# Ending the local softmax inside its own attention step, with the exponentials ahead of the probability transposes

## The chip, the cores and the metric

One Trainium2 chip, one core of it. The metric is the device time of one launch, in microseconds, as the median of several runs; lower is better. A profile is one further execution, taken by the hardware profiler.

## The reference

An attention layer of 4 batches, 8 heads, 576 positions and head dimension 64 is followed by two mixture-of-experts layers on its 2304 rows of 512 numbers. The attention has two parts that are added: a local one, in which a position sees the positions less than 4 away, and a coarse one on means over 4 positions.

```python
q_d = q.reshape(B, H, Sd, 4, D).mean(axis=3)            # k_d and v_d alike, Sd = 144
out_up = np.repeat(sm_attn(q_d, k_d, v_d), 4, axis=2)
mask = np.abs(pos[:, None] - pos[None, :]) < 4
scores = np.where(mask, scale * q @ k.T, -1e9)
attn = softmax(scores)                                   # denominators get + 1e-9
x = out_up + attn @ v                                    # then two MoE layers, top 2 and top 1
```

## The kernel before

The program is written for a manual schedule: each engine executes its instructions in the order in which the Python code issues them. It has an attention stage, a short passage to the experts, and the two expert layers, which are almost all matrix multiplication.

The attention runs as a software pipeline over 16 pairs of heads, in a loop of 18 steps (L1104). In step i it works on four pairs at once. In the order of issue:

- `transposes(i+1)`: TensorE turns queries and keys (tiles `pq`, `pk`); VectorE sums them over 4 positions (`qd`, `kd`), ScalarE copies them out (`qT`, `kT`).
- `softmax2(i-1)`: VectorE sums the local exponentials (`sm`) and takes reciprocals, for the coarse sums (`smd`) too; GpSimd multiplies three of the four bands into the block matrix `Pd`, VectorE one; GpSimd scales the coarse probabilities `ped`.
- `values(i-2)` on TensorE (tiles `pva`, `pvm`), and `scale_d`, ScalarE's copy `od`.
- In some steps `xback_att` (tile `px`), which turns 128 finished rows back. It stands ahead of the scores in steps 6, 7, 10, 11, 14 and 15 and at the end of steps 6, 7, 9, 10, 11, 13 and 14.
- `scores(i)`: 90 small matmuls into the tile `pd`, local ones first, coarse ones last. Then `combine(i-2)` on VectorE (`xT`).
- `p_transposes(i-1)`, first half: TensorE turns the 10 blocks of `Pd` into three tiles `pp`, which ScalarE copies to `pT`.
- `softmax1(i)`: VectorE takes the maximum `mx` and subtracts it (`pe`), ScalarE takes the exponential.
- `p_transposes(i-1)`, second half: 8 transposes of `ped` into two tiles `ppd`, and their copies `pdT`.
- `softmax_d1(i)`, in every second step `group(g+1)` (tile `prs`), and `softmax_d2(i)`: the coarse maximum `mxd` on VectorE and four exponentials on ScalarE.
- `pool_v`: three additions on GpSimd for the coarse values `vd`.

The tiles `pq`, `pk`, `pva`, `pvm`, `pp`, `ppd` and `prs` all come from one pool of PSUM with four buffers (tag `P`), so each one has to wait for the readers of the tile that was taken four places before it:

```python
self.ps = ctx.enter_context(tc.tile_pool(name="attP", bufs=4, space=PSUM))   # L63
pp = self.ps.tile([128, 4, 128], F32, tag="P", name="pp")                    # L281
```

Score tiles and `px` share a second pool of two. From step 12 on, the first router's work on VectorE, GpSimd and TensorE (`route1`) is fed in between: every VectorE instruction of the attention is followed by `tick(1)`, which issues the router's next piece, such as the comparisons `ol` (L526, GpSimd) and `oh` (L527, VectorE), which the matmuls of L532 multiply. After step 17 come the last five `px`, their stores to DRAM, and the first expert.

Of the kernel before, what the change touches and what calls it, by code (L numbers as in the profile page):

```python
# [15 lines left out]
ALU = mybir.AluOpType  # L16
# [28 lines left out]
class Attention:  # L45
# [208 lines left out]

    def softmax2(self, i):
        nc, NB, W, KW, sb = self.nc, self.NB, self.W, self.KW, self.sb
        st = self.st[i]
        pe, ped, smd = st["pe"], st["ped"], st["smd"]
        Pd = self.Pd[i % 2]
        sm = sb.tile([128, 2 * NB], F32, tag="sm", name="sm")  # L260
        self.V.tensor_reduce(sm, pe, axis=AX.X, op=ALU.add)
        self.V.tensor_scalar(sm, sm, 1e-9, None, op0=ALU.add)
        self.V.reciprocal(sm, sm)
        self.V.tensor_scalar(smd, smd, 1e-9, None, op0=ALU.add)
        for g in (1, 2, 3, 0):
            n = KW if g < 3 else W
            s = slice(W * g, W * (g + 1))
            eng = self.V if g == 0 else nc.gpsimd
            eng.tensor_tensor(Pd[s, :, W * g:W * g + n], pe[s, :, :n],  # L269
                              sm[s, :, None].to_broadcast([W, 2 * NB, n]), op=ALU.mult)  # L270
        self.V.reciprocal(smd, smd)
        nc.gpsimd.tensor_tensor(ped, ped, smd[:, :, :, None].to_broadcast([72, 2, 2, self.Sd]), op=ALU.mult)

# [99 lines left out]
def finish_now(gen):  # L373

    while True:
        try:
            next(gen)
        except StopIteration as e:
            return e.value
# [155 lines left out]
class Items:  # L535
# [87 lines left out]
    def next(self):  # L623

        nc, w, tag, nt = self.nc, self.consts, self.tag, self.nt
        m = w.tile([128, self.most], F32, tag=f"{tag}nm", name="nm")
        j = w.tile([128, self.most], F32, tag=f"{tag}nj", name="nj")
        r = w.tile([128, 1 + nt], F32, tag=f"{tag}nr", name="nr")
        ei = w.tile([128, 1], I32, tag=f"{tag}nei", name="nei")
        nc.vector.tensor_scalar(m, self.ij, self.count, None, op0=ALU.is_equal)  # L630
        for a, src in enumerate([self.ei] + [self.col[:, a] for a in range(nt)]):
            nc.vector.tensor_tensor(j, m, src, op=ALU.mult)
            nc.vector.tensor_reduce(r[:, a:a + 1], j, axis=AX.X, op=ALU.add)
        nc.vector.tensor_copy(ei, r[:, 0:1])
        nc.vector.tensor_scalar(self.count, self.count, 1.0, None, op0=ALU.add)
        return dict(e=ei[0:1], e128=r[:, 0:1], col=[r[:, 1 + a:2 + a] for a in range(nt)])
# [219 lines left out]
def core(ctx, tc, q, k, v, moe_w_gate, moe_w_noise, moe_noise, moe_w1, moe_w2,  # L856
         moe2_modality_id, moe2_w_gate, moe2_modality_bias, moe2_w1, moe2_w2, out):
    nc = tc.nc
# [40 lines left out]
    with ExitStack() as actx:  # L899
        att = Attention(actx, tc, q, k, v, identF, xpool)  # L900
# [64 lines left out]
        def flush():  # L965
            while after:
                after.pop(0)()

        def xback_att(t):
            px = att.psD.tile([128, 2, 512], F32, tag="D", name="px")  # L970
            pv = px[:, :, :2 * XB].rearrange("p a (b c) -> p a b c", b=2)
            xr = xback(t, [pv[:, 0], pv[:, 1]])

            def rest():
                nc.scalar.activation(xr, pv[:, :, :, :128], AF.Copy)
                lgs = axr.tile([128, 2, 2, 2 * E], F32, tag="lgs", name="lgs")
                nc.scalar.activation(lgs, pv[:, :, :, 128:], AF.Copy)
                nc.vector.tensor_reduce(lg[:, t], lgs.rearrange("p a b c -> p c a b"), axis=AX.XY, op=ALU.add)
                nc.scalar.dma_start(x_rows[128 * t:128 * t + 128, :DM], xr.rearrange("p a b c -> p (a b c)"))
            after.append(rest)  # L980
# [62 lines left out]
        def tick(n=1, pe=False):  # L1043

            if pe:
                wait[0] = False
            while n and back and not wait[0]:
                n -= 1
                try:
                    what = next(back[0])  # L1050
                    wait[0] = what in ("PE", "PE soon") and not pe
                    age[0] = 2 if what == "PE soon" else 0
                except StopIteration:
                    back.pop(0)

        def unblock(lag=0):

            if wait[0]:
                if age[0] < lag:
                    age[0] += 1  # L1060
                else:
                    wait[0] = False
                    tick(1)
# [20 lines left out]
        def places_early():  # L1084

            v, f = (t.rearrange("p (e t) -> p e t", e=E)[:, :NX, :NE0] for t in (tab, fs))
            yield from rt.decode(f, v, rt.padh.rearrange("p (e t) -> p e t", e=E)[:, :NX, :NE0])
            nc.vector.tensor_copy(idx0[:, 0], f)

            d = route.tile([128, NX, NE0], F32, tag="hold2", name="hold2")  # L1090
            nc.vector.tensor_scalar(d, f, float(N), -float(N), op0=ALU.is_ge, op1=ALU.mult)
            yield
            nc.vector.tensor_tensor(idx0[:, 1], d, f, op=ALU.add)
            yield

        att.tick = tick
        NP = 4 * B
# [6 lines left out]
        for i in range(NP + 2):  # L1104
            g, ph = divmod(i, 2)
            if ph == 1:
                if g + 1 < 2 * B:
                    att.load_vr(g + 1)
                if g + 2 < 2 * B:
                    att.load_qk(g + 2)  # L1110
            if ph == 0 and i and g < 2 * B:
                att.load_vw(g)
            if 3 <= i <= 7:
                next(small, None)
            if i == NP - 1:
                att.pool_v(g, 1)
            if i + 1 < NP:
                if i == 0:
                    att.scores(i)
                    att.softmax1(i)  # L1120
                tr = att.transposes(i + 1)
                next(tr)
            if 1 <= i <= NP:
                att.softmax2(i - 1)
            if i + 1 < NP:
                finish_now(tr)
            if i >= 2:
                att.values(i - 2)
                att.scale_d(i - 2)
            flush()  # L1130
            if i == 12:
                back.append(route1(0, HT, att_bank, nc.vector, nc.gpsimd, hold))
                back.append(places_early())
            unblock(1)
            if i in before:
                xback_att(before[i])
            if 0 < i < NP:
                att.scores(i)
            if i >= 2:
                att.combine(i - 2)  # L1140
            flush()
            tick(2)
            if 1 <= i <= NP:
                pt = att.p_transposes(i - 1)
                next(pt)
            if 0 < i < NP:
                att.softmax1(i)
            if 1 <= i <= NP:
                finish_now(pt)
            unblock(1)  # L1150
            if i < NP:
                att.softmax_d1(i)
                if ph == 0 and g + 1 < 2 * B:
                    att.group(g + 1)
                att.softmax_d2(i)
                for c in ((0,), (1,))[ph] if i > 1 else ((), (0, 1))[ph]:
                    if i < NP - 1:
                        att.pool_v(g, c)
            tick(2 if i < NP else 30)
            if i == 9:  # L1160
                second_bias()
            if i in behind:
                xback_att(behind[i])
            if i == 12:

                nc.sync.dma_start(x_rows[N:].rearrange("(a p) c -> p a c", p=128),
                                  zero[:, None, :].to_broadcast([128, 5, XW]))
            if i == 14:
                ffn.begin([dict(e=e, ns=n, w1=moe_w1, w2=moe_w2) for e, n in
                           [(e, EARLY) for e in range(NX)] + [(e, 640 - EARLY) for e in range(NX)]  # L1170
                           + [(e, 640) for e in range(NX, E)]]
                          + [dict(ns=n, w1=moe2_w1, w2=moe2_w2) for n in [512, 256, 256, 384] + [256] * (STATIC - 1)])

                nc.sync.dma_start(x2_rows.rearrange("(a p) c -> p a c", p=128),
                                  zero[:, None, :YW].to_broadcast([128, NT + 5, YW]))
# [490 lines left out]
```

## Time and profile before

| what | value |
|---|---|
| median of 3 runs | 917.04 us (916.91 to 917.12) |
| the profiled execution | 912.9 us, span 911.2 us |
| TensorE busy in the span | 861.5 us (95%) |
| VectorE, ScalarE, GpSimd busy | 544.4, 431.3, 324.7 us |
| attention (to about 163 us): TensorE, VectorE, ScalarE, GpSimd busy | 137.36, 123.70, 98.16, 121.95 us |
| mean granted TensorE clock | 0.981 of 2.4 GHz |

Busy time is the time in which an engine executes. The profiled execution is one of its own, 4.1 us below the median of the runs. A wait is put down to the engine and the line whose result came last.

### The profile page before, as it was taken

What the parts mean: (1) busy time and instruction counts of PE and PEld (TensorE: products, weight loads), DVE (VectorE), ACT (ScalarE), POOL (GpSimd) and SP (SyncE); (2) the same over time, 40 slices, a digit from 0 to 9 for tenths busy, and PEclk for the clock granted to TensorE, in tenths of its full rate; (3) what the DMA queues carried; (4) which work ended last, traced back from release to release, by engine and by line L of the source; (5) the groups of instructions that cost most, each with busy time, mean ns of one, the idle gap of its engine ahead of it and who ended that gap; (6) DMA issues with size and microseconds to landing.
All of it is one profiled execution on the core that took longest, in us unless ns stands there. A gap on an engine that the chain in (4) does not pass through costs nothing. (4 is left out here: it accounts for less than half of the span.)

```text
span 911.2 us, 18186 instructions
## 1 busy us (share of the span) xinstructions
PE 861.5 (95%) x6775; PEld 757.3 (83%) x6775; DVE 544.4 (60%) x1317; ACT 431.3 (47%) x967; POOL 324.7 (36%) x460
## 2 busy tenths in 40 slices
PE   5898987799999999999999999989989999999995
PEld 4777876688889989999999989978867889999995
DVE  5776887489865544553343443434666877556662
ACT  3676764455554434443342333334324456455562
POOL 7767768265532304224015051050020442222210
PEclk9999998899999999999999999999999999999998
DMA  7978897675776647466237264184424477556660
GB/s 167 178 149 200 203 287 248 205 227 159 247 240 170 162 142 204 122 210 160 74 99 162 88 110 148 47 191 157 147 63 131 142 249 244 185 179 214 212 208 24
DMA packets 158701, 153.82 MB, mean 169 GB/s; under 512 B 74319, under 2 KB 119887, under 8 KB 158608
## 3 DMA queue, kind: packets, MB, share of 16 engines
q1 hardware_dynamic: 142336, 113.33, 41.0%
q0 software_dynamic: 12080, 32.45, 15.5%
q10 hardware_dynamic: 4192, 6.82, 2.1%
q8 instruction: 56, 0.92, 0.4%
q14 instruction: 37, 0.30, 0.1%
HBM read 124.98 MB, written 27.85 MB: 168 GB/s over the span
## 5 line engine op out<-in xcount | busy, mean ns | idle before, releaser
L728 PE MATMUL ph<-xh,whi 128*128 128x256 f32 (+3 forms) x768 | 238.3, 310 | 4.6 <-ACT xh L713 2.4
L728 PE MATMUL ph<-xl,whi 128*128 128x256 f32 (+3 forms) x768 | 237.3, 309 | 0.5 <-DVE xl L714 0.5
L728 PE MATMUL ph<-xh,wlo 128*128 128x256 f32 (+3 forms) x768 | 237.3, 309 | 0.4 <-DVE wlo L689 0.3
L740 PE MATMUL y<-whi,hh 128*128 128x512 f32 x472 | 191.0, 405 | 0.0
L689 DVE TENSOR_TENSOR wlo<-raw,whi 128x512 fp32r<-128x512 f32 x135 | 93.3, 691 | 158.7 <-ACT whi L688 146.0
L740 PE MATMUL y<-wlo,hh 128*128 128x512 f32 x472 | 187.0, 396 | 0.0
L740 PE MATMUL y<-whi,hl 128*128 128x512 f32 x472 | 186.4, 395 | 0.1
L688 ACT ACTIVATE whi<-raw 128x512 fp32r<-128x512 f32 x160 | 101.0, 631 | 167.6 <-PE y L740 149.8
L728 PEld LDWEIGHTS ph<-xh,whi 128*128 128x128 f32 x768 | 145.7, 190 | 14.1 <-ACT xh L713 3.1
L728 PEld LDWEIGHTS ph<-xl,whi 128*128 128x128 f32 x768 | 145.7, 190 | 8.4 <-DVE xl L714 1.1
L730 ACT ACTIVATE hh<-ph 128x256 fp32r<-128x256 f32 (+3 forms) x192 | 83.3, 434 | 141.0 <-PE ph L728 130.2
L728 PEld LDWEIGHTS ph<-xh,wlo 128*128 128x128 f32 x768 | 145.8, 190 | 2.3 <-DVE wlo L689 0.8
L731 DVE SCALAR_TENSOR_TENSOR hl<-ph,hh 128x256 fp32r<-128x256 f32 (+3 forms) x192 | 92.5, 482 | 85.0 <-ACT hh L730 82.4
L1208 POOL DMA_INDIRECT x_rows<-y,idx x35 | 57.8, 1652 | 207.3 <-ACT y L1199 107.3
L691 DVE TENSOR_TENSOR wlo<-raw,whi 128x512 fp32r<-128x512 f32 x160 | 119.4, 746 | 12.5 <-ACT whi L690 11.3
L740 PEld LDWEIGHTS y<-whi,hl 128*128 128x128 f32 x472 | 88.8, 188 | 21.6 <-DVE wlo L691 0.5
L740 PEld LDWEIGHTS y<-whi,hh 128*128 128x128 f32 x472 | 89.4, 189 | 13.2 <-DVE y L1201 0.2
L690 ACT ACTIVATE whi<-raw 128x512 fp32r<-128x512 f32 x160 | 98.7, 617 | 1.9 <-DMA raw<-in_moe_w_dram 1.9
L740 PEld LDWEIGHTS y<-wlo,hh 128*128 128x128 f32 x472 | 89.2, 189 | 12.5
L714 DVE TENSOR_TENSOR xl<-pt,xh 128x512 fp32r<-128x512 f32 x59 | 38.6, 687 | 33.3 <-ACT xh L713 33.1
L1208 POOL DMA_INDIRECT out_dram<-y,pi x19 | 20.6, 1085 | 99.7 <-ACT y L1199 43.9
L269 POOL TENSOR_TENSOR Pd<-pe,sm 32x380 f32<-32x380 f32 (+1 forms) x48 | 42.4, 884 | 31.4 <-DVE smd L40 19.5
(304 smaller groups left out, 1073.8 us busy)
## 6 DMA issues: line engine op xcount, KB each, us to landing
raw<-in_moe_w_dram SPq DMA_DIRECT2D x156, 512.0 KB
x_rows<-zero SPq DMA_DIRECT2D x1, 5934.0 KB
vr<-in_v_dram SPq DMA_DIRECT2D x16, 288.0 KB
x2l<-x_rows SPq DMA_DIRECT2D x18, 256.0 KB
qk<-in_q_dram SPq DMA_DIRECT2D x32, 128.0 KB
qk<-in_k_dram SPq DMA_DIRECT2D x32, 128.0 KB
x_rows<-xr ACTq DMA_DIRECT2D x13, 256.0 KB
vw<-in_v_dram SPq DMA_DIRECT2D x24, 128.0 KB
```

Of the source, the lines that this page charges most:

```text
L269: eng.tensor_tensor(Pd[s, :, W * g:W * g + n], pe[s, :, :n], sm[s, :, None].to_broadcast([W, 2 * NB, n]), op=ALU.mult)
L688: nc.scalar.activation(h1, a, AF.Copy)
L689: eng.tensor_tensor(l1, a, h1.bitcast(F32), op=ALU.subtract)
L690: nc.scalar.activation(hi[:, 1], r2[:, half], AF.Copy)
L691: nc.vector.tensor_tensor(lo[:, 1], r2[:, half], hi[:, 1].bitcast(F32), op=ALU.subtract)
L714: nc.vector.tensor_tensor(xl, p, xh.bitcast(F32), op=ALU.subtract)
L728: nc.tensor.matmul(ps, w[a][:, k], x[b][:, k, s], start=(i == 0), stop=(i == 3 * KD - 1))
L730: nc.scalar.activation(hh[:, s], ps, AF.Relu)
L731: nc.vector.scalar_tensor_tensor(hl[:, s], ps, 0.0, hh[:, s].bitcast(F32), op0=ALU.max, op1=ALU.subtract)
L740: nc.tensor.matmul(p, h[a][:, 128 * j:128 * j + 128], w[b], start=(f == 0 and i == 0), stop=(f == self.FB - 1 and i == 2))
L1208: d = nc.gpsimd.indirect_dma_start(out=dst, out_offset=bass.IndirectOffsetOnAxis(ap=ix, axis=0), in_=y, in_offset=None, **kw)
```

## The change

The local part of `softmax2`, which stood near the beginning of the next step, is issued at the end of its own step, behind `softmax_d1`. What it did for the coarse part becomes a function of its own, which stays near the beginning of the next step. `softmax1` is issued ahead of the whole of `p_transposes`, so that on ScalarE the local exponential of pair i stands ahead of the copies `pT` of pair i-1. `pool_v` moves from the end of a step to a place behind the scaling of `ped`.

```diff
     def softmax2(self, i):
...
         self.V.reciprocal(sm, sm)
-        self.V.tensor_scalar(smd, smd, 1e-9, None, op0=ALU.add)
         for g in (1, 2, 3, 0):
...
+
+    def softmax_d3(self, i):
+        nc = self.nc
+        ped, smd = self.st[i]["ped"], self.st[i]["smd"]
+        self.V.tensor_scalar(smd, smd, 1e-9, None, op0=ALU.add)
         self.V.reciprocal(smd, smd)
         nc.gpsimd.tensor_tensor(ped, ped, smd[:, :, :, None].to_broadcast([72, 2, 2, self.Sd]), op=ALU.mult)
...
-            if i == NP - 1:
-                att.pool_v(g, 1)
...
             if 1 <= i <= NP:
-                att.softmax2(i - 1)
+                att.softmax_d3(i - 1)
+            if 0 < i < NP:
+                for c in ((0,), (1,))[ph] if i > 1 else (0, 1):
+                    att.pool_v(g, c)
...
             tick(2)
+            if 0 < i < NP:
+                att.softmax1(i)
             if 1 <= i <= NP:
                 pt = att.p_transposes(i - 1)
                 next(pt)
-            if 0 < i < NP:
-                att.softmax1(i)
             if 1 <= i <= NP:
                 finish_now(pt)
             unblock(1)
             if i < NP:
                 att.softmax_d1(i)
+                att.softmax2(i)
                 if ph == 0 and g + 1 < 2 * B:
                     att.group(g + 1)
                 att.softmax_d2(i)
-                for c in ((0,), (1,))[ph] if i > 1 else ((), (0, 1))[ph]:
-                    if i < NP - 1:
-                        att.pool_v(g, c)
```

## Rows read from the trace of the kernel before

**Rows 1.** Busy us (x instructions) of PE, PEld, DVE, ACT, POOL; clock, DMA share, GB/s.
```profile
0.00:163.00 163.00, 137.36 (x2525) 117.40 (x2525) 123.70 (x345) 98.16 (x330) 121.95 (x182) 0.96 0.83 205
...
180.00:911.00 731.00, 712.02 (x4182) 629.09 (x4180) 414.28 (x959) 326.78 (x624) 199.28 (x266) 0.99 0.54 160
```
**Rows 2.** Waits of TensorE, 12 to 145 us: total, times, longest.
```profile
PE pp L283 <- POOL Pd L269: 9.0, 8, 2.4
...
PEld prs L166 <- ACT pT L284: 0.6, 2, 0.4
```
**Rows 3.** Timeline of step 3 (start us, duration us, engine, line).
```profile
31.07 0.66 PE L193 MATMUL pq<-gw,qk 128*128 128x128 f32 x4
...
34.42 2.77 POOL L269 TENSOR_TENSOR Pd<-pe,sm 32x380 f32<-32x380 f32 x3 [2.22 <-DVE smd L40]
...
37.25 1.31 PE L283 MATMUL pp<-gw,Pd 128*128 128x128 f32 x10 [1.55 <-POOL Pd L269]
...
39.09 0.66 PE L193 MATMUL pq<-gw,qk 128*128 128x128 f32 x4
```
**Rows 4.** Timeline of step 7: its beginning and its last part.
```profile
64.06 0.60 PE L193 MATMUL pq<-gw,qk 128*128 128x128 f32 x4
...
68.84 0.71 PE L222 MATMUL pd<-kd,qd 64*72 64x144 f32 x8
69.49 1.31 PE L283 MATMUL pp<-gw,Pd 128*128 128x128 f32 x10
69.60 0.55 DVE L40 TENSOR_REDUCE mx<-pd 128x10 f32<-128x380 f32 x1 [0.66 <-PE pd L222]
...
70.26 0.55 DVE L40 TENSOR_TENSOR pe<-pd,mx 128x380 f32<-128x380 f32 x1
...
70.63 0.67 PE L292 MATMUL ppd<-gw,ped 72*72 72x72 f32 x8
...
71.14 1.19 PE L955 MATMUL px<-gw,xT 128*128 128x144 f32 x8
...
71.36 0.53 ACT L233 ACTIVATE pe<-pe 128x380 f32<-128x380 f32 x1
...
71.77 0.71 ACT L294 ACTIVATE pdT<-ppd 72x288 f32<-72x288 f32 x2
```
**Rows 5.** Instructions that write `pT`: duration in ns, min/median/max.
```profile
L284 ACT ACTIVATE pT<-pp x48: 367/571/580, 20.8 to 153.4; 128x488 f32<-128x488 f32 x32, 128x244 f32<-128x244 f32 x16
```
**Rows 6.** Busy time and granted clock (PEclk) by stretch of the attention.
```profile
64.10:72.20 8.10, 8.10 (x162) 7.35 (x161) 6.67 (x18) 5.92 (x22) 5.37 (x7) 1.00 0.75 151
31.00:106.10 75.10, 69.06 (x1395) 59.12 (x1393) 57.16 (x145) 51.52 (x182) 55.52 (x70) 1.00 0.86 184
111.10:123.60 12.50, 9.69 (x166) 8.06 (x167) 12.36 (x38) 6.74 (x22) 8.70 (x11) 0.93 0.88 241
121.90:125.30 3.40, 3.40 (x21) 3.37 (x19) 3.33 (x10) 1.52 (x4) 2.31 (x4) 0.50 0.81 178
```
**Rows 7.** Timeline of steps 1 and 2.
```profile
19.63 2.40 PE L283 MATMUL pp<-gw,Pd 128*128 128x128 f32 x10 [3.59 <-DVE mxd L40]
...
25.45 0.47 PE L309 MATMUL pva<-pdT,vd 72*64 72x144 f32 x4 [1.16 <-POOL vd L181]
```
**Rows 8.** Timeline of steps 12 and 13, with the router's work in between.
```profile
120.90 1.97 PE L283 MATMUL pp<-gw,Pd 128*128 128x128 f32 x10 [2.39 <-POOL Pd L269]
...
123.58 0.54 DVE L40 TENSOR_REDUCE mx<-pd 128x10 f32<-128x380 f32 x1
...
124.95 0.52 ACT L233 ACTIVATE pe<-pe 128x380 f32<-128x380 f32 x1 [1.64 <-DVE pe L40]
...
125.49 0.60 PE L193 MATMUL pq<-gw,qk 128*128 128x128 f32 x4
```
**Rows 9.** Timeline of the change from step 15 to step 16.
```profile
146.07 0.69 ACT L294 ACTIVATE pdT<-ppd 72x288 f32<-72x288 f32 x2
...
146.51 1.28 PE L309 MATMUL pva<-pdT,vd 72*64 72x144 f32 x7 [2.02 <-ACT pdT L294]
```

More of the change, by code (lines that the diff above doesn't have):

```diff
@@ L256, in softmax2 @@
         nc, NB, W, KW, sb = self.nc, self.NB, self.W, self.KW, self.sb
-        st = self.st[i]
-        pe, ped, smd = st["pe"], st["ped"], st["smd"]
+        pe = self.st[i]["pe"]
         Pd = self.Pd[i % 2]
```

## The prediction

> **What bounds the kernel now.** I read the busy time by stretch first. From 180 us to the end TensorE is busy 712 of 731 us [rows 1], and the change touches nothing there: whatever the attention gains or loses arrives at the end unchanged. In the attention TensorE idles 26 of 163 us [rows 1]; that is all there is to win. The table of waits says for what it idles: 9.0 us, eight times, for `Pd` from GpSimd [rows 2]. The timelines show the place. In step 3 `pq` starts at 31.07; its sum `qd` and, behind it in VectorE's queue, the sums and reciprocals of `softmax2` let GpSimd start `Pd` only at 34.42, 2.77 long; `pp` starts at 37.25 after 1.55 idle, and the next `pq` at 39.09 [rows 3]. So the loop is `pq`, `qd`, `sm`, `Pd`, `pp`, `pq`: 8.02 us. Steps that also carry `px` have the extra matmuls to hide it: from 64.1 to 72.2 TensorE is busy all the time [rows 6]. Over steps 3 to 11 (31.0 to 106.1) it idles 75.1 - 69.06 = 6.0 us in nine steps [rows 6].
>
> **The change part by part.**
>
> *What it removes.* `Pd` of pair i is started by GpSimd at the end of step i. It needs 2.8 us, and the next step's `pp` comes only after transposes, values and scores, over 4 us of TensorE. All waits of `pp` for `Pd` go, and those for `vd`, as `pool_v` comes earlier in the step. No instruction is added or taken away: the same three `Pd` products, one `ped` product and three additions of `pool_v`, the same VectorE instructions and ticks, the same DMAs. SP's queue keeps its order; `pool_v` ends earlier, so buffers for the next `vr` come free earlier, not later.
>
> *What it adds.* On ScalarE the exponential of pair i now stands ahead of the copies `pT` of pair i-1, and it waits for scores, maximum and subtraction of pair i. Queued behind it: three `pT`, two `pdT`, the four coarse exponentials, the next `kT`, `qT`, `od`. TensorE waits for these through the four PSUM buffers. The order in the pool is `pq pk pva pvm pp pp pp ppd ppd` (`prs`): the second `ppd` takes the buffer of the first `pp`, so it waits for the first `pT`; the next `pq` waits for the second `pT` (behind a `prs`, for the third). That the pool works so is seen now: `prs` waited for `pT` twice [rows 2].
>
> *The new wait, from step 7* [rows 4]. Let S be the end of the scores, 68.84 + 0.71 = 69.55. `mx` starts 0.05 later, `pe` 0.66 after it, 0.55 long; the exponential could start at S + 1.3 (now it starts at 71.36 because the copies are ahead of it). The next ScalarE instruction starts 0.41 after an exponential (71.36 to 71.77), and a first `pT` takes 0.57 [rows 5]: done at S + 2.3, so the second `ppd` starts at S + 2.35. TensorE is there at S + 1.4: `pp` at 69.49, `ppd` at 70.63, half of which is 0.3. It stalls 0.95 us, or 1.05 where `pq` or `prs` follows at once and waits for the next copy. The price falls in every step, also in those in which TensorE never waited. It lies between nothing (other work ready in the queue: there is none, the queue is in order) and this 0.95 to 1.05.
>
> *Is something else the loop then?* From S: stall and `ppd` to S + 2.7, `pq` at S + 2.8 (S + 3.2 with `prs`), and from `pq` to the next S 4.5 us (64.06 to 69.55 is 5.5, with 1.1 of `px` [rows 4]). That is 7.3 and 7.7 us against 8.02 now in step 3. ScalarE's chain from the exponential to `od`, and `combine` behind it, comes to S + 7.1 or 7.4, just inside. So the plain steps gain a little and the steps with `px` lose.
>
> *Sum, in the profiled execution's time.*
> Steps 0 to 2: `pp` waits 3.59 now [rows 7]; `Pd` can start about 1 us earlier, as the two sums of `group` and one `qd` (0.7) no longer stand ahead of it on VectorE. GpSimd's queue is full behind it, so the `vd` for which `values` of step 2 wait [rows 7] comes 1 us earlier too, and the new stall takes most of that: -0.2 (bounds -1.5 to +0.5).
> Steps 3 to 11: nine stalls, 9.2 us in all, for 6.0 of idle now: +3.1; the `vd` waits stretch some matmuls that count as busy, three times about 0.3: +2.1 (bounds -1.5, with half the stall, to +3.1).
> Steps 12 and 13: between the two maxima of pairs 12 and 13 VectorE is busy 12.36 of 12.50 us [rows 6], and its instructions between them are the same before and after, with as many ticks. So the second maximum doesn't come earlier. Now `pq` starts 1.91 after it (123.58 to 125.49), as `pp` and most of `ppd` are done [rows 8]. After the change the second `ppd` waits for it: exponential at +1.37 [rows 8], `pT` done at +2.35, then 0.3 and a `px` of 1.1 us: `pq` at +3.8, or 1.9 later. TensorE would stand idle for about 5 us ahead of that. After the idle of 2.39 us at this place the granted clock was 0.50, that is 1.2 GHz, for 3.4 us [rows 6, 8]; then it fell on `pp` and `ppd` ahead of the maximum, and would now fall on `px` behind it, another 1.3. I take +2.5 (bounds 0 and +3.2).
> Step 14: the router's matmuls stand behind the `ppd` and come 1.1 us later; VectorE waits for them: +1.1 (bounds 0 and +1.1).
> Steps 15 to 17: the first `pva` waits 2.02 us for `pdT` [rows 9], which now is next behind the exponential on ScalarE; with three `pT` between (1.2 us) it starts that much later. The router's last comparisons on GpSimd wait for matmuls behind that `pva`: +1.1 (bounds -3, if GpSimd, relieved of one `Pd`, ends earlier, and +1.2).
> Together -0.2 + 2.1 + 2.5 + 1.1 + 1.1 = +6.6: 912.9 becomes 919.5. The median of the runs is 4.1 above the profiled execution: 923.6.
>
> *The skill.* The rows show one wait of TensorE repeating from step to step, for `Pd` [rows 2, 3], and a full pool behind it only as 0.6 us. The Trainium skill, Perfetto Trace Analysis, Optimization Strategy, says that a gap which keeps repeating on the engine that should be saturated can mean that there is not enough PSUM for the next tile. The trace doesn't bear this out for the kernel before; it would for the one after. The same section also advises to make the producer of such a gap start sooner: by that alone the gaps are gain and the time is the 907 of the first rival.
>
> **The rivals.**
> *Faster: the stall at the second `ppd` does not come.* It decides at one point: whether the first `pT` is done by S + 1.4. That needs a pool that gives the second `ppd` a free buffer. For it: the waits for `Pd` are real, and the step would then be limited by the rest of the loop. Gain: 9.0 for `Pd` in eight places [rows 2], 1.2 for `vd` [rows 7], 1.7 for 3.4 us at half clock, less about 2 that ScalarE's chain keeps: 10, so 907. Against it: the wait of `prs` for `pT`.
> *No change: the stall comes, the router's steps don't lose.* VectorE is what sets steps 12 to 16 (12.36 of 12.50); if TensorE's lateness is caught up there, as the next maximum waits for VectorE anyway, only -0.2 + 2.1 remain, and a GpSimd that ends earlier in the tail gives some of it back: about 917 to 919. For it: VectorE idles little; against it: the maximum of pair 14 waits for TensorE.
> *Slower still: the longer idles cost the clock in several places*, each 1.7 us as in the 3.4 us at 0.50 [rows 6], in steps 13, 15 and 16: 928.
>
> **How the numbers follow.** Forecast, +3 to +9: 0.56, time 923.6, its own range 920 to 926. Faster rival: 0.24 (the waits removed are measured, the added one is derived). No change: 0.15. Slower still: 0.05. A difference under 0.2%, 1.8 us, can't be told from none with this kernel's runs. The forecast and the slowest case make slower 0.61, and 0.01 of the middle case joins them; 0.13 of the middle case is within the bound and 0.01 below it: faster 0.25, same 0.13, slower 0.62. The range leaves out the better half of the faster rival: 908 to 928.
>
> **What would show it.** In the profile after: no wait of `pp` for `Pd`; instead `ppd` waiting for `pT`, about 0.9 us in nearly each of 15 steps; `pT` starting right behind the exponential; TensorE idle in each of steps 6, 7, 10 and 11, which have none or little now; the distance of `pq` to `pq` near 7.3 in steps 3 and 5 and above 9 in step 7; after the maximum of pair 13 `pq` over 3.5 us later. The prediction is wrong if `ppd` waits for nothing, or if VectorE reaches the second maximum of the router's steps earlier than 12.5 us after the first.

## The result, and the profile after

The median went from 916.77 us (16 runs) to 921.38 us (16 runs): ratio 1.0055, 95% interval 1.004 to 1.0069, so the change costs about 5 us of 917. That lies in the forecast's own range of 920 to 926. The profiled execution after took 921.21 us (span 919.5), the one before 912.9 (span 911.2).

The two profiled executions therefore differ by 8.3 us where the medians differ by 4.6. That of after lies at its median, that of before 3.9 under its own. A stage's loss in the table further down is a difference of these two executions, and 3.7 us of all the losses together are chance that can't be put into one stage.

TensorE's waits after, from 12 to 150 us (total, times, longest; the view of [rows 2]):

```profile
PE ppd L295 <- ACT pT L287: 13.3, 14, 2.7
PE pp L286 <- DVE kd L40: 2.1, 1, 2.1
PE pva L312 <- POOL vd L181: 2.0, 1, 2.0
```

The 9.0 us of waits for `Pd` [rows 2] are gone, and 13.3 us of waits for `pT` stand in their place: one of 0.84 us in nearly every step, and a long one among the router's work. The waits removed were eight; those added are fourteen. Step 7, with `px`, the counterpart of [rows 4], shows one of them being made:

```profile
71.72 0.56 DVE L40 TENSOR_REDUCE mx<-pd 128x10 f32<-128x380 f32 x1 [0.66 <-PE pd L222]
71.77 1.15 PE L286 MATMUL pp<-gw,Pd 128*128 128x128 f32 x9
...
72.38 0.55 DVE L40 TENSOR_TENSOR pe<-pd,mx 128x380 f32<-128x380 f32 x1
...
72.75 0.41 PE L295 MATMUL ppd<-gw,ped 72*72 72x72 f32 x4
...
72.97 0.52 ACT L233 ACTIVATE pe<-pe 128x380 f32<-128x380 f32 x1 [2.20 <-DVE pe L40]
73.39 1.29 ACT L287 ACTIVATE pT<-pp 128x488 f32<-128x488 f32 x3
...
74.01 0.45 PE L295 MATMUL ppd<-gw,ped 72*72 72x72 f32 x4 [0.84 <-ACT pT L287]
...
74.29 1.19 PE L958 MATMUL px<-gw,xT 128*128 128x144 f32 x8
...
74.88 1.97 POOL L267 TENSOR_TENSOR Pd<-pe,sm 32x380 f32<-32x380 f32 x2 [3.16 <-DVE sm L40]
...
75.32 0.60 PE L193 MATMUL pq<-gw,qk 128*128 128x128 f32 x4
```

Read it along one matrix. `mx` and `pe` run on VectorE while TensorE transposes `pp` and the first half of `ppd`. ScalarE idles 2.20 us, since the exponential heads its queue and has no input yet; only behind it, at 73.39, does the first `pT` copy start, though its `pp` had long been written. The second half of `ppd` waits for that copy, `px` and the next `pq` stand behind it on TensorE. `Pd` is now made at the end of the step, in good time.

The busy windows answer [rows 1] and the last lines of [rows 6] (busy us of PE, PEld, DVE, ACT, POOL; clock, DMA share, GB/s):

```profile
0.00:163.00 163.00, 132.61 (x2450) 112.08 (x2452) 119.85 (x327) 92.66 (x316) 116.35 (x176) 0.95 0.80 200
180.00:919.50 739.50, 721.05 (x4239) 637.45 (x4238) 419.32 (x969) 331.23 (x634) 198.59 (x267) 0.99 0.53 161
...
114.50:127.20 12.70, 9.40 (x176) 7.55 (x170) 12.37 (x39) 5.58 (x20) 7.93 (x10) 1.00 0.75 213
128.40:135.00 6.60, 6.16 (x38) 5.83 (x40) 3.59 (x12) 4.41 (x17) 4.06 (x5) 0.50 0.98 306
```

TensorE is as full behind 180 us as before (97.5% after, 97.4% before), so the loss is the attention's; there it idles 30 us of the first 163 instead of 26. Among the router's steps VectorE is again full (12.37 of 12.70), and then come 6.6 us at a granted clock of 0.50, 1.2 GHz, against 3.4 us in [rows 6]. They begin at the end of this wait, the counterpart of [rows 8]:

```profile
126.43 0.54 DVE L40 TENSOR_REDUCE mx<-pd 128x10 f32<-128x380 f32 x1
...
128.22 1.29 ACT L287 ACTIVATE pT<-pp 128x488 f32<-128x488 f32 x3
...
128.84 0.70 PE L295 MATMUL ppd<-gw,ped 72*72 72x72 f32 x4 [2.68 <-ACT pT L287]
...
129.32 2.22 PE L958 MATMUL px<-gw,xT 128*128 128x144 f32 x8
...
131.34 1.06 PE L193 MATMUL pq<-gw,qk 128*128 128x128 f32 x4
```

Here `px` took 2.22 us where it takes 1.19 at the full clock (71.14 in [rows 4]), and `pq` came 4.9 us behind the maximum; before, 1.91 [rows 8]. But before, this `px` had run in the slow stretch too: it started at 123.62 and took 2.03 us. Of the 3.0 us by which `pq` comes later, 2.85 are the wait of `ppd` and its transposes, and 0.15 the longer `px`.

By stages, from the same marks in both traces (start of `pq`, of `mx`, of the last block of `px`):

| stage | before, us | after, us | difference | forecast |
|---|---|---|---|---|
| to `pq` of step 3 | 31.07 | 34.09 | +3.0 | -0.2 |
| `pq` of step 3 to `pq` of step 12 | 75.06 | 76.69 | +1.6 | +2.1 |
| `pq` of 12 to `pq` of 14 | 19.36 | 20.56 | +1.2 | +2.5 |
| `pq` of 14 to `mx` of pair 15 | 18.94 | 18.66 | -0.3 | +1.1 |
| `mx` of 15 to the last `px` block | 12.31 | 16.06 | +3.7 | +1.1 |
| behind it | 754.46 | 753.44 | -1.0 | 0 |

The middle came as forecast or milder; the two ends, which the forecast had nearly level, lost most. How far one trace can be trusted is seen where others have the same instructions: steps 3 to 11, issued in the same order as after, take 76.68, 76.71 and 78.16 us in three kernels of the experiments below, and 72.84 and 74.58 in a pair of kernels that differ from each other only in the steps behind. The stretch behind the last `px` lies between 752.8 and 757.2 us in all of them, so the -1.0 of the last row is within chance.

### The profile page after: what moved, and what is told of

Its sections match the earlier page's. It is cut to its first block, busy times and chain, and to the rows that moved or that the text cites. A ratio compares the mean times of both kernels' runs of the same rounds, so it can differ in the third digit from the quotient of the medians.

```text
span 919.5 us, 18177 instructions
## 1 busy us (share of the span) xinstructions
PE 864.8 (94%) x6775; PEld 758.8 (83%) x6775; DVE 546.2 (59%) x1317; ACT 430.9 (47%) x967; POOL 322.7 (35%) x460
## 5 line engine op out<-in xcount | busy, mean ns | idle before, releaser
L743 PEld LDWEIGHTS y<-wlo,hh 128*128 128x128 f32 x472 | 89.3, 189 | 12.7
```

What stands on the lines that cost most here:

```text
L743: nc.tensor.matmul(p, h[a][:, 128 * j:128 * j + 128], w[b], start=(f == 0 and i == 0), stop=(f == self.FB - 1 and i == 2))
```

## The experiments

Each ratio is to the kernel before, run beside it on the same chip.

**Which half of the change costs: two experiments that undo one half each.** The first takes the kernel before and only puts the exponential ahead of the transposes:

```
             flush()
             tick(2)
+            if 0 < i < NP:
+                att.softmax1(i)
             if 1 <= i <= NP:
                 pt = att.p_transposes(i - 1)
                 next(pt)
-            if 0 < i < NP:
-                att.softmax1(i)
```

> The kernel before with one part of the change alone: the local maximum, subtraction and exponential ahead of the transposes of probabilities; the local softmax still ends in the next step. Pool theory (the second ppd waits for the first copy pT, which now stands behind the exponential): where pp waits for Pd anyway, as in steps 3 and 5, little changes; in steps 6, 7, 10, 11 and 14, which had no wait, about 0.9 us of TensorE's waiting for pT appears, and in steps 13 to 16 some 4 us: 6 to 9 us slower than before, about 0.8%. Rival (the loss comes from the moved softmax2 and pool_v, which load VectorE and GpSimd at other moments): this part alone costs nothing, within 0.2% of before.

Measured: 924.42 us, ratio 1.0085 (1.0063 to 1.0108).

```profile
PE ppd L292 <- ACT pT L284: 9.3, 9, 2.7
PE pp L283 <- POOL Pd L269: 6.0, 7, 1.3
```

The wait for `pT` comes with the new order alone, without any other part of the change. So over the whole kernel the moved softmax part is not what costs; in the full change it seems to take back about 3 us of these 8 (the two intervals overlap a little). The tail, below, is another matter.

The second takes the kernel after and puts `p_transposes` ahead of `softmax1` again (the same lines, the other way round):

> The changed kernel with the copies pT put back ahead of the local exponential; softmax2 stays at the end of its own step. Pool theory: no ppd waits for pT any more. Three copies end 1.9 us after the scores, so the exponential starts 0.5 us later than in the changed kernel; GpSimd's Pd then ends some 6.3 us after the scores, and the next pp comes 6.2 us after them at the earliest: waits of pp for Pd of at most 0.2 us. Steps 3 and 5 shrink to about 6.4 us, nine steps 3 to 11 lose their 6 us of idle: 6 to 9 us faster than before, about 909 where before has 917. Rival (moved work is what costs): no faster than before, and the waits of TensorE turn up for Pd, with 1 us or more in each step.

Measured: 914.66 us, ratio 0.9991 (0.9971 to 1.001).

```profile
PE pva L312 <- POOL vd L181: 3.5, 3, 2.0
PE pvm L318 <- DVE qd L40: 3.1, 2, 2.7
```

Up to 150 us no `ppd` waits for `pT` and no `pp` for `Pd`, and the kernel is level with the one before. But the gain of 6 to 9 us over the kernel before, which should then have been there, isn't. In its trace steps 3 to 11 take 72.7 us, 2.3 less than before, with 3.2 us of them at a clock of 0.53 (79.5 to 82.7, behind a wait of 1.53 us for a load of q); and the last stage takes 17.9 us instead of 12.3, with the last `Pd` 7.3 us behind `mx` of pair 15 (148.90 and 141.58). What the steps win, the tail more than gives back.

**The move of `pool_v`.** The kernel after with the additions of `vd` at their old place, at the end of the step (the last ones at the beginning of step 15):

```
+            if i == NP - 1:
+                att.pool_v(g, 1)
...
-            if 0 < i < NP:
-                for c in ((0,), (1,))[ph] if i > 1 else (0, 1):
-                    att.pool_v(g, c)
...
                 att.softmax_d2(i)
+                for c in ((0,), (1,))[ph] if i > 1 else ((), (0, 1))[ph]:
+                    if i < NP - 1:
+                        att.pool_v(g, c)
```

> The changed kernel with pool_v back at its old places (end of the step; for the last pair of heads the beginning of step 15). In the profile of the changed kernel GpSimd idles 7.15 us ahead of Pd of pair 14, and then ped, pool_v and five comparisons of the router stand ahead of Pd of pair 15, for which pp waits 1.3 us. If the place of pool_v is what costs the 3.7 us that are lost between the maximum of pair 15 and the last px, 2 to 3 us come back: 918.5 where before has 917. The pool theory alone says that ppd goes on waiting 0.84 us for pT in each step and that steps 3 to 11 keep their length (76.7 us).

Measured: 958.66 us, ratio 1.046 (1.0437 to 1.0482); the expectation was far off.

```profile
PE pva L312 <- POOL vd L181: 22.7, 7, 4.1
PE ppd L295 <- ACT pT L287: 6.1, 8, 0.9
```

At their old place the additions now stand behind this step's `Pd` on GpSimd, and `Pd` there waits for the exponential, so `values` of the next step waits for `vd`. Moving `softmax2` up with `pool_v` left at this place is no option.

**The buffer by itself.** If TensorE is tied to the exponential only because the second `ppd` takes the buffer of the first `pp`, then using one buffer less must free it, with the order on ScalarE as it is. The first of the four coarse blocks goes into the free columns of the third `pp`, the other three into one `ppd` (`coarse` makes the two transposes of one block):

```
+            if n == 2:
+                one = pp.rearrange("p a b -> p (a b)")[:72, 256:400]
+                coarse(one, 0, 0)
             nc.scalar.activation(pT[:, m0:m0 + n], pp[:, :n, :self.QB], AF.Copy)
...
+        nc.scalar.activation(pdT[:, 0, 0], one, AF.Copy)
+        pq = self.ps.tile([128, 512], F32, tag="P", name="ppd")
+        pv = pq[:72, :432].rearrange("p (c q) -> p c q", c=3)
+        for j in range(3):
+            coarse(pv[:, j], (j + 1) // 2, (j + 1) % 2)
```

> Kernel after with its order untouched (exponential ahead of the copies), but the transposes of the coarse probabilities use one PSUM buffer less: the first of their four blocks goes into the free columns of the third pp buffer, the other three into one ppd buffer. So no ppd takes the buffer that the first pT copy empties. Theory (the PSUM buffer is what ties TensorE to the exponential): the waits of ppd for pT (13.3 us over 14 steps) vanish and the plain steps fall from 7.28 and 7.68 us to 6.5 to 7.0; ratio 0.993 to 0.999. Rival 1 (ScalarE's order itself is the cost, because pva needs pT and pdT): a wait of pva or of the next pq for ScalarE of 0.5 to 1 us per step takes its place, ratio 1.003 to 1.006. Rival 2 (TensorE's next bound is GpSimd or VectorE): waits vanish but half of the gain only, ratio 0.999 to 1.002.

> Control: kernel before with the packed PSUM buffers alone. In its order the copies stand ahead of the exponential, so there is no wait of ppd for pT to take away (0.6 us in all). Theory: ratio 0.998 to 1.002, or slower by up to 0.3%, since the third pT copy now also waits for ped, which GpSimd finishes 1.15 us behind Pd. Rival (one buffer more in the ring is worth something in any order): 0.992 to 0.996.

Measured: the kernel after so packed 916.60 us, ratio 1.0006 (0.9986 to 1.0026); the kernel before so packed 914.01 us, 0.9975 (0.9956 to 0.9995). Waits of the former:

```profile
PE prs L166 <- ACT pT L296: 4.9, 6, 1.4
PE pq L193 <- ACT pT L296: 2.8, 3, 1.6
...
PE pva L318 <- POOL vd L181: 1.9, 2, 1.4
```

All waits of `ppd` for `pT` are gone with the exponential still ahead of the copies, and steps 3 to 11 fall from 76.69 to 72.84 us. So the wait was one for a buffer. A part of it comes back one tile later: `prs` and `pq` take the buffers that the later copies empty, 7.7 us in nine places. That is between the theory and the first rival, and the time is that of the second. The control is slightly better than the kernel before, just below what was expected; its trace doesn't show where (steps 3 to 11 take 75.17 us, 0.1 more). Beside that control the packed change is no gain, rather a small loss.

**Coarse part first.** The kernel after, with the transposes and copies of `ped` ahead of the exponential and `pp`, `pT` behind it:

```
-        pT = self.sb.tile([128, 2 * NB, self.QB], F32, tag="pT", name="pT", bufs=1)
...
-        yield
         pdT = self.sb.tile([72, 2, 2, self.Sd], F32, tag="pdT", name="pdT", bufs=1)
...
             nc.scalar.activation(pdT[:, h], pv, AF.Copy)
+        yield
+        pT = self.sb.tile([128, 2 * NB, self.QB], F32, tag="pT", name="pT", bufs=1)
...
+            if 1 <= i <= NP:
+                pt = att.p_transposes(i - 1)
+                next(pt)
             if 0 < i < NP:
                 att.softmax1(i)
```

> The changed kernel with the transposes of the coarse probabilities and their copies pdT issued ahead of the local softmax1; pp and pT come behind it as in the changed kernel. The order in the pool becomes pq pk pva pvm ppd ppd pp pp pp, so nothing that TensorE does before the second tile of the next step waits for pT. Pool theory: the 0.84 us at ppd is gone. But GpSimd scales ped only behind Pd, some 7.2 us after the scores of its step, and the coarse transposes come 6.2 us after them: ppd waits for ped by up to 1 us in steps without px, not in those with px. 2 to 5 us faster than before, 913 where before has 917, and slower than the kernel with the copies first. Rival (moved work costs): as slow as the changed kernel, 921.

Measured: 913.17 us, ratio 0.9967 (0.995 to 0.9985): faster than both kernels.

```profile
PE ppd L287 <- POOL ped L275: 13.3, 10, 3.8
```

The stall moved to `ped`, as expected (13.3 us is by chance also the sum of the waits for `pT` after), and steps 3 to 11 take 72.5 us. If GpSimd's chain were the bound, one quarter of `Pd` moved to VectorE should bring much of the 13.3 us:

```
-            eng = self.V if g == 0 else nc.gpsimd
+            eng = self.V if g in (0, 3) else nc.gpsimd
```

> Coarse order as before, and one of GpSimd's three quarters of Pd put on VectorE beside the one it has. What the coarse order still pays is the wait of ppd for ped (13.3 us over ten steps), and ped stands on GpSimd behind three quarters of Pd of 0.92 us each. Theory A (GpSimd's chain sets the steps): ped comes 0.9 us earlier per step, the waits fall by 5 to 9 us, ratio to before 0.988 to 0.993. Theory B (VectorE, at 0.54 us more per step, is the bound in the steps where it has no idle time, two of four): steps 6, 7, 10, 11, 13 and 14 get longer by 0.5 us each and the waits move to pe and mx; ratio 0.996 to 1.003.

Measured: 913.51 us, ratio 0.9976 (0.9958 to 0.9993).

```profile
PE ppd L287 <- POOL ped L275: 6.5, 4, 3.5
PE pvm L318 <- DVE qnl L994: 2.8, 1, 2.8
```

Half of the wait goes and nothing is won: steps 3 to 11 take 73.3 us, 0.8 more. The time is that of theory B, and the waits that come in place of those for `ped` are for VectorE (2.6 us for `qd` in four places, where it was 2.1 in one, and the 2.8 for `qnl`). But of the steps that theory B named only 7, 11, 13 are longer (0.45, 0.46 and 0.75 us); 6 and 10 are shorter (1.3 and 0.4). That VectorE is the next bound fits the trace, and is not shown step by step.

**The tail.** GpSimd after, from pair 14 to pair 15:

```profile
144.16 2.83 POOL L267 TENSOR_TENSOR Pd<-pe,sm 32x380 f32<-32x380 f32 x3 [7.15 <-ACT ped L251]
147.09 3.53 POOL L529 TENSOR_SCALAR ol<-r_h,lclo 128x128 f16<-128x128 f16 x5
150.59 1.19 POOL L275 TENSOR_TENSOR ped<-ped,smd 72x576 f32<-72x576 f32 x1
151.74 0.72 POOL L181 TENSOR_TENSOR vd<-vr 72x256 f32<-72x256 f32 x1
152.53 1.53 POOL L181 TENSOR_TENSOR vd<-vd,vr 72x256 f32<-72x256 f32 x2
154.04 3.20 POOL L529 TENSOR_SCALAR ol<-r_h,lclo 128x128 f16<-128x128 f16 x5
157.33 2.49 POOL L267 TENSOR_TENSOR Pd<-pe,sm 32x380 f32<-32x380 f32 x3
```

It idles 7.15 us and then has no gap: the last additions of `vd` and the router's `ol` stand ahead of the last `Pd`, which starts 7.3 us after `mx` of pair 15 (150.00). Before, it was 3.1:

```profile
144.43 0.49 DVE L40 TENSOR_REDUCE mx<-pd 128x10 f32<-128x380 f32 x1
...
147.57 2.83 POOL L269 TENSOR_TENSOR Pd<-pe,sm 32x380 f32<-32x380 f32 x3 [0.87 <-DVE sm L40]
```

Three kernels make those additions one step earlier, in the idle time: one on the kernel after, one on the coarse order and one on the packed kernel:

```
-            if 0 < i < NP:
-                for c in ((0,), (1,))[ph] if i > 1 else (0, 1):
+            if 0 < i < NP - 1:
+                for c in ((0,), (1,))[ph] if 1 < i < NP - 2 else (0, 1):
```

> Kernel after, but the last four additions of vd (heads of the last group, second half) are done in step 14 beside the first half instead of in step 15. Theory (GpSimd's queue in the tail): in the kernel after, the additions of 2.25 us stand on GpSimd between ped of step 14 (150.59) and Pd of step 15 (157.33), and before that GpSimd was idle for 7.15 us; moved into that idle time they let Pd of step 15 start some 2 us earlier, the 1.30 us wait of pp at 159.87 goes, and the last block of px starts 1 to 2.3 us earlier: ratio to before about 1.003 to 1.0045 where the kernel after had 1.0055. Rival (the tail is late because VectorE hands its softmax over late, and the GpSimd order is only what shows it): Pd of step 15 then waits for sm on VectorE instead, and the time stays at 1.0055 within 0.001.

> Both together: transposes and copies of the coarse probabilities ahead of the exponential, the fine ones behind it, and the last additions of vd in step 14. Theory: the PSUM wait goes to ped (13 us over ten steps, shorter each than the exponential's) and the tail gains 1 to 2.3 us more: ratio to before 0.994 to 0.996 where the coarse order alone had 0.9967. Rival (tail set by VectorE): 0.9967 within 0.001.

> Packed PSUM and the last additions of vd in step 14. Theory: both gains add, some 1 us below the packed kernel, ratio 0.992 to 0.998. Rival (the tail's gain came from GpSimd time that the packed kernel has elsewhere): equal to the packed kernel within 0.001.

Measured: 919.89 us, ratio 1.0044 (1.0027 to 1.0061); 910.92 us, 0.9947 (0.9925 to 0.997); and, on the packed kernel, 912.62 us, 0.9967 (0.995 to 0.9984). In the first of them:

```profile
145.41 3.58 POOL L529 TENSOR_SCALAR ol<-r_h,lclo 128x128 f16<-128x128 f16 x5
148.96 1.14 POOL L275 TENSOR_TENSOR ped<-ped,smd 72x576 f32<-72x576 f32 x1
150.09 3.17 POOL L529 TENSOR_SCALAR ol<-r_h,lclo 128x128 f16<-128x128 f16 x5
153.34 2.49 POOL L267 TENSOR_TENSOR Pd<-pe,sm 32x380 f32<-32x380 f32 x3
```

The last stage falls from 16.06 to 13.66 us in the kernel after, from 15.85 to 13.58 in the coarse order, from 17.32 to 13.60 in the packed one: 2.3 to 3.7 us in three pairs. The ratios follow with 0.0011, 0.0020 and 0.0039, that is 1.0, 1.8 and 3.6 us; only in the packed pair are the intervals apart, so it is the traces together that carry this. The other traces agree: that stage takes 15.8 to 17.9 us in all that have these additions ahead of the last `Pd`, but for one; 12.1 to 12.7 in those with GpSimd's old order; and the one, with a quarter of `Pd` moved to VectorE, takes 13.65, as GpSimd has less to do there too. The coarse order with the early additions is the best of all, 0.5% under the kernel before; its lead over the plain coarse order is within the intervals.

**The start.** First the order: steps 0 to 2 as before, the change from step 2's `Pd` and step 3's exponential on.

```
+            if 1 <= i <= 2:
+                att.softmax2(i - 1)
...
-            if 0 < i < NP:
+            if 2 < i < NP:
                 att.softmax1(i)
...
-                att.softmax2(i)
+                if i > 1:
+                    att.softmax2(i)
```

(`pool_v` of the first group and the exponentials of pairs 1 and 2 go back to their old places as well.)

> Kernel after, but steps 0 to 2 keep the order of the kernel before (Pd of a step at the start of the next one, additions of vd behind it, transposes of probabilities ahead of the exponential); the change starts with Pd of step 2 and the exponential of step 3. Theory (of the 3.0 us that the start lost, some 1.9 are the new order, 1.1 a VectorE cast that took 2.40 us by chance): the transposes of step 3 start at 31 to 32.5 instead of 34.09, and the time falls by 1 to 2.5 us: ratio to before 1.003 to 1.0045. Rival (the start is late by the cast alone): the transposes of step 3 start 2.9 to 3.1 us after the first softmax of step 2 as in the kernel after whatever the order, and the ratio stays 1.0055 within 0.001.

Measured: 922.32 us, ratio 1.006 (1.0038 to 1.0082); `pq` of step 3 at 33.42. The theory falls: the old order brings 0.7 us of the 3.0. The rival, the chance cast, falls too: here and in the kernel with the early additions, whose first steps are those of the kernel after, the cast took 1.30 us, and `pq` of step 3 stands at 33.42 and 33.79. The window shows something else:

```profile
20.90:31.00 10.10, 9.07 (x135) 7.40 (x134) 5.07 (x10) 4.43 (x17) 9.34 (x13) 0.50 0.78 166
```

TensorE ran for 10.1 us at the lower clock, through `values`, scores and transposes of step 2. TensorE's order there is that of the kernel before, and `vd` came at the same time:

```profile
25.43 0.75 PE L312 MATMUL pva<-pdT,vd 72*64 72x144 f32 x4 [1.02 <-POOL vd L181]
...
33.42 0.66 PE L193 MATMUL pq<-gw,qk 128*128 128x128 f32 x4
```

From `vd` to `pq` that is 7.99 us at a mean clock of 0.64; before, 5.62 at 1.00 (25.45 in [rows 7] to 31.07 in [rows 3]), and in neither does TensorE wait in between. So these 2.4 us are the clock's. Next, the wait for `vd` in that step, 2.01 us after and 1.16 before [rows 7]. The last kernel leaves out two of the three additions of each `vd` of the first group, so that group's coarse values are those of one row in four:

```
-        for part in range(3):
+        for part in range(3 if g else 1):
```

> Kernel after, but for the first group of heads two of the three additions of each vd are left out (its coarse values are those of one row in four), so vd is ready 3.0 us earlier in step 1; for the rest it is the kernel after. Theory (the start is lost to the 2.01 us wait of pva for vd in step 2, and to the TensorE clock of 0.50 that the trace shows behind it): no wait of pva for vd, clock 1.00 in most of 24 to 31, transposes of step 3 at 30 to 31.5 instead of 34.09, and the time some 2.5 to 3.5 us less, ratio 1.002 to 1.003. Rival (VectorE, without idle time from 14.2 to 25.7, sets step 2): transposes of step 3 at 33 or later, ratio 1.0045 to 1.0055.

Measured: `pq` of step 3 at 32.71, between the two expectations; no wait for `vd`, but this:

```profile
21.90:28.70 6.80, 6.80 (x122) 5.81 (x122) 3.76 (x10) 3.90 (x15) 5.98 (x8) 0.51 0.87 181
```

Without the wait 1.4 of the 3.0 us are back; the clock was low even so. The run's ratio of 1.0056 (921.27 us) is that of the kernel after, though in the trace the last `px` block comes 2.7 us earlier (163.32 instead of 166.06). What took these back isn't shown: the stretch behind, 756.3 us, is within the spread of the other traces, and with other values tokens may also go to other experts.

## Why the prediction came out right, and where its sum was off

**The wait removed and the wait added** were as forecast. Every wait of `pp` for `Pd` up to 150 us went; one of 1.30 us came at 159.87, in the tail. Not as forecast, `values` of step 2 goes on waiting for `vd`, 2.01 us instead of 1.16. The second `ppd` waits for the first `pT` in every step from 3 to 12 and in 14, 0.84 us where 0.95 was worked out, and the plain steps take 7.28 and 7.68 us (34.09 to 41.37 to 49.05) where 7.3 and 7.7 stood; step 7 takes 9.15 (66.17 to 75.32) where "above 9" stood. That it is a matter of a buffer, and not of ScalarE's order as such, is shown by the packed kernel, which keeps the order and loses the wait; that the order of the copies makes it, by the two half changes. The forecast had said that the rule of the Trainium skill would hold for the kernel after: the trace of after shows the same gap of 0.84 us in step after step, and packing the buffers took it away. So it agrees with the Trainium skill, Perfetto Trace Analysis, Optimization Strategy, that repeating gaps can mean too little PSUM.

**Steps 3 to 11**, term +2.1: +1.6 between the two profiled executions. Right.

**Steps 12 and 13**, term +2.5: +1.2. The place was right: `ppd` waits 2.68 us, the clock falls to 0.50, and `pq` comes 3.0 us later behind the maximum. Of the two parts the wait was sized too small and the slow `px` too large, since that `px` was slow before as well; the sum of both, 3.2, was near. What failed is the step "so the second maximum doesn't come earlier": VectorE needed 11.17 us between the two maxima (115.26 to 126.43) instead of 12.5, so 1.3 us came back ahead of the wait. The prediction named this as a sign of being wrong, and for this term it was one. The instructions were the same, as forecast, but not their durations. One of them before, beside GpSimd's `Pd`, and the same one after, with GpSimd idle:

```profile
118.14 2.71 POOL L269 TENSOR_TENSOR Pd<-pe,sm 32x380 f32<-32x380 f32 x3 [3.25 <-DVE qnl L993]
119.29 0.84 DVE L465 TENSOR_TENSOR tpk<-qnl,tpm 128x72 f32<-128x72 f32 x1
```

```profile
123.29 0.23 DVE L468 TENSOR_TENSOR tpk<-qnl,tpm 128x72 f32<-128x72 f32 x1
```

Five instructions are 0.5 to 0.8 us longer before, three others 0.4 to 0.6 longer after, and each of these eight lies beside an instruction of GpSimd, which is busy for 8.70 us between the maxima before and 6.53 after. No run varied this alone.

**Step 14**, term +1.1: -0.3. VectorE did get the router's matmuls later, 10.55 us behind `pq` of step 14 instead of 8.78. But from there to the maximum of pair 15 it took 8.11 us instead of 10.16 (GpSimd busy 5.62 instead of 9.71), so the lateness didn't reach that maximum.

**The tail**, term +1.1, bounds -3 to +1.2: +3.7, outside the bounds. The later `pva` came as forecast (3.55 us behind `mx` of pair 15, 153.55, instead of 2.08). The step that failed is "GpSimd, relieved of one `Pd`, ends earlier", and with it the sum's silence on `pool_v`: moving it took it past `softmax2` in GpSimd's queue, and in step 15 this put 2.25 us of additions, and the router's `ol` behind them, ahead of the last `Pd`. Early additions took back 2.3 to 3.7 us in three kernels; on the kernel after they left +1.35, near the forecast's +1.1.

**The start**, term -0.2, bounds -1.5 to +0.5: +3.0. The step "the `vd` comes 1 us earlier too" holds where the cast is short: in the kernel with the early additions `vd` was ready at 24.72, 0.7 before the 25.45 of [rows 7]. What failed is the unspoken step behind it, that from there on step 2 runs as before but for the stall. From that point to `pq` of step 3 it took 5.62 us before, 8.28 after, 9.07 with the early additions. The window of that last kernel, and the same window of the packed kernel:

```profile
24.60:31.00 6.40, 6.28 (x119) 5.21 (x120) 1.41 (x4) 0.29 (x1) 5.70 (x8) 0.50 1.00 195
```

```profile
24.60:31.00 6.40, 5.20 (x134) 4.47 (x134) 3.69 (x8) 1.76 (x6) 5.89 (x8) 1.00 1.17 216
...
25.71 0.47 PE L318 MATMUL pva<-pdT,vd 72*64 72x144 f32 x4 [1.38 <-POOL vd L181]
...
32.03 0.66 PE L193 MATMUL pq<-gw,qk 128*128 128x128 f32 x4
```

The packed kernel keeps the order of the kernel after and has a stall of the same size (0.65 us, of `prs` for `pT`, where `ppd` waits 0.67), and the clock was 1.00, as in the kernel before. It took 6.32 us (25.71 to 32.03), and 6.32 again when packed and with the early additions, where `vd` came at 24.71. So of the 3.45 us between 5.62 and 9.07 some 0.7 go with the stall and 2.75 with the clock; the kernel with the old order in its first steps puts the clock at 2.4. For the kernel after, whose stall is 0.90, that leaves about 1.8 us of clock: an estimate from these traces. The stall was in the sum; a slow stretch over `values` and scores was the term put at nothing. Why the clock fell there in some kernels and not in the packed ones, no run shows.

**From the profile to the median.** The sum gave +6.6 in profiled time, and 4.1 were added on the ground that the profile of before was faster than its median. Of after it was not: its profile lies at its median. The two errors, a sum 1.7 us too small and an offset 3.9 too large, left the forecast 2.2 us too high. That the total fell into the range is in part luck: the two ends lost 5.8 us more than their terms, steps 3 to 14 3.2 us less, and 1.0 us more came back behind them. The new wait itself was no luck: it is there in each step, with its size. But the buffer is not all that costs: beside the packed kernel before (0.9975) the packed change is still 0.3% slower (1.0006), with a last stage of 17.3 us, and only with the early additions as well is it level (0.9967).

**The gain that didn't come.** With the wait removed in three other ways steps 3 to 11 take 72.5 to 72.8 us, 2.2 to 2.6 less than before (74.6 in one more trace of the packed order, with some 3 us at the lower clock from 80 on): that, and not the 5.4 us of waits for `Pd` in these steps, is what the earlier softmax is worth there. So the faster rival's gain of 10 us doesn't come even with its condition met: the packed kernel is level with the kernel before. The next waits are for VectorE's `qd`, GpSimd's `ped` or the later copies. The tail then gave it back unless `pool_v` was moved on.

## What to carry to other kernels

When an instruction is moved ahead of another on an in-order engine, list what the overtaken one frees: here copies that empty PSUM, and through a rotating pool a tile of another name, four allocations on, waited for an exponential it never reads. Waits of 5.4 us in nine steps were worth 2.2 to 2.6 us: look up which engine is full in the same steps. And that the same instructions take the same time is an assumption of its own: here VectorE was 1.3 us faster over the same ones. Last, check the first and the last two steps of a pipelined loop apart from the middle: this loop's steady steps were forecast to 0.5 us, its ends to about 3.

## What the runs showed of the hardware that was not expected

Where a stretch at the lower clock falls mattered more here than its length. In steps 1 and 2 the trace of every kernel here has one. Before, it followed the 3.59 us of [rows 7] and lay from 19.2 to 22.9 (mean 0.54), over `pp`, `ppd` and `pq`, with the wait for `vd` still to come, which would have been longer without it. After, it followed the wait for `vd` itself and lay from 25 to 29 (mean 0.61), on matmuls that nothing could cover; these 14 of `pvm` took 1.04 us before:

```profile
25.81 0.70 PE L312 MATMUL pva<-pdT,vd 72*64 72x144 f32 x4 [2.01 <-POOL vd L181]
...
27.00 1.91 PE L318 MATMUL pvm<-pT,vw 128*64 128x122 f32 x14
```

And one instruction of the start, VectorE's cast of `mask` beside GpSimd's memsets of `Pd`, took 1.30 us in ten profiles and 2.40 us in four (of the kernel after among them), one or the other and nothing between. Of the 1.1 us only 0.3 were left at `pq` of step 3 in the kernel after (34.09, and 33.79 with the same first steps), but 1.0 in the packed pair (32.03 and 31.03).
